# A hand-written start of a gated-attention and SiLU kernel: two weight pieces asked for ahead of the fourth chunk's loads, that chunk's transposes behind the third's scores, and two roundings ahead of Silus

## Chip, cores and metric

The kernel runs on one core of one Trainium2 chip. The metric is device time in microseconds (us), the median of several executions. The five engines of the core are named as in the profile: PE (TensorE; PEld are its weight loads), DVE (VectorE), ACT (ScalarE), POOL (GpSimd) and SP (SyncE, which here issues most DMAs; SPq are its issues).

## What is computed

A gated recurrence over 768 tokens for 4 x 8 heads of 48 columns, then a feed-forward block with SiLU over all 3072 tokens:

```python
batch, n_heads, seq, head_dim = (4, 8, 768, 48)
...
for t in range(S):
    state = alpha[:, :, t, :, None] * state + np.einsum('bhd,bhe->bhde', k[:, :, t], v[:, :, t])
    y[:, :, t] = np.einsum('bhd,bhde->bhe', q[:, :, t], state)
...
x = np.ascontiguousarray(attn_out.transpose(0, 2, 1, 3)).reshape(B * S, H * D)
...
h = x @ w_in                           # 3072x384 @ 384x2048
g = h * (1.0 / (1.0 + np.exp(-h)))
return (g @ w_out).astype(np.float32)  # 2048x384
```

Both weights arrive in 8-byte numbers, so the kernel reads them as pairs of 32-bit words ("bits") and makes single-precision weights of them itself.

## The kernel before

**Chunks.** The recurrence is worked in chunks of 128 tokens of one batch, all heads together; there are 24 (chunk 0 to 3 are the first 128 tokens of the four batches, chunk 4 starts the second 128 of batch 0). A chunk goes through these steps:

- `load(n)` (line 480) has SP issue three DMAs of 192 KB: alpha, k and q of the chunk (tiles `an`, `kn`, `qn`) into one of two sets of buffers, by n even or odd. `load_v(n)` (510) does the same for v (`vn`, two buffers).
- `bring(n)` (726) has PE transpose alpha, k and q, four transposes each, into PSUM, and ACT copies alpha's out (line 749, tile `al`). Alpha's bank, and from chunk 4 on k's and q's too, come from a pool of three, `ps_a`.
- `products(n)` (751) is DVE's part: two scans and two multiplies make the scaled k (`kp`) and q (`qp`, tile `p`).
- `scores(n)` (819) is 16 small matmuls into two banks of `ps_a`. ACT copies both out (line 844, tile `g`), POOL blanks the upper triangle (845), and `back` (871) transposes `kp` on PE, with a copy by ACT (881).
- `values(n)` (883) multiplies g with v, and ACT copies the result to `xt` (903), the input of the feed-forward block. `states(n)` (904) makes the state.

**Weights.** The 12 pieces of w_in (512 KB each) and then the 16 of w_out are fetched in order. `fetch()` (527) takes one of four buffers and has SP issue the DMA (533). `weights()` (629) turns one piece into single precision each time it is called: DVE, in three instructions (660, 662, 663), puts the number together, with a rounding that ACT has made ahead of it (644). Having done piece i, it issues the rounding of piece i + 1 on ACT and fetches piece i + 4. So each call to `w(upto)` in `start()` puts pieces through until `upto` of them are done. The buffer of piece i + 4 is that of piece i, which is free once DVE's line 662 and ACT's rounding have read it.

**Feed-forward block.** `go_on()` (1198) takes the next unit of work from a list. The first units are those of `enter_plain` (951): 12 matmuls of 128x256 with two column blocks of w_in into one of three banks (`ps_m`), then one Silu by ACT (963). The first four use pieces 0 to 5, the fifth and sixth pieces 6 to 8, and the seventh needs pieces up to 11.

**The order.** In `start()` (1237), which the change edits, the order of all this for the first chunks is written out by hand. The flag `stated` is on while it runs: PE's matmuls and transposes, the loads and fetches of SP, and ACT's roundings, Silus and copies are then kept in program order, each within its engine (lines 381 to 394). So what stands earlier in `start()` is issued earlier on each engine that it uses, and an instruction that waits holds up what follows on its own engine. After `start()`, a loop over steps with `fill` (1224) brings the remaining chunks and units.

Of the kernel before, what the change touches and what calls it, by code (L numbers as in the profile page):

```python
# [355 lines left out]
def quotients(  # L356
# [30 lines left out]
    def settled(ins):  # L387

        return tc.keep_in_program_order(ins) if stated[0] else ins
# [48 lines left out]
    def out_bank(i, n):  # L438
        return outs[i].tile([128, 512], F32, name="ps_o")[:, 0:n]

    def ps_attn(n=C):
        return ps_a.tile([128, 512], F32, name="ps_a").rearrange("p (j c) -> p j c", c=n)
# [4 lines left out]
    def idle(n):  # L447

        for _ in range(n):
            pe.matmul(spin[:, 0:C], lhsT=ident, rhs=ident, start=True, stop=True)  # L450
# [17 lines left out]
    NIN = 2  # L468
# [11 lines left out]
    def load(n, names="akq"):  # L480
        if n == NT:
            return
        c = ctxs.setdefault(n, dict(zip(("ci", "b"), divmod(n, B))))
        b, rows = c["b"], slice(c["ci"] * C, c["ci"] * C + C)
        for name, src in (("a", alpha), ("k", k), ("q", q)):
            if name not in names:
                continue
            x = src[b, :, rows, :]
            if n < NA:
                c[name] = nat[name][n % NIN]  # L490
                settled(nc.sync.dma_start(c[name][:, :, 0:D], x.transpose([1, 0, 2])))
                continue

            c[name] = late["quads"][name]
            for u in range(2):
                for i in range(2):
                    r = 64 * u + 32 * i
                    nc.sync.dma_start(  # L500
                        c[name][r : r + 32, 32 * (1 - i) :][:, 0 : 4 * NP * D].rearrange(
                            "p (g c) -> p g c", g=NP),
                        x[u::2].rearrange("h (b j) d -> b h (j d)", j=4))

    NV = 2
# [4 lines left out]
    def load_v(n):  # L510
        c = ctxs.setdefault(n, dict(zip(("ci", "b"), divmod(n, B))))
        x = v[c["b"], :, c["ci"] * C : c["ci"] * C + C, :].transpose([1, 0, 2])
        t = c["v"] = vns[n % NV]
        if n < NA:
            settled(nc.sync.dma_start(t[:, :, 0:D], x))
            return
        nc.sync.dma_start(t[:, 0 : H // 2, 0:D], x[:, 0 : H // 2])
        for e in range(2):
            nc.sync.dma_start(t[CH * e : CH * e + CH, H // 2 :, 0:D], x[CH - CH * e : C - CH * e, H // 2 :])
# [198 lines left out]
    def tokens(t):  # L718

        return t[:, 1 : NP * W + 1].rearrange("p (j c) -> p j c", c=W)[:, :, 0:C]  # L720

    def turned(x, to):
        x = x[:, 32:].rearrange("p (g j d) -> p g j d", j=4, d=D)
        dve.transpose(to.rearrange("p g (b j) -> p g j b", j=4), x[:, :, :, 0:32])

    def bring(n, names="akq"):

        c = ctxs[n]
        sg = seg[0 if late else n % 2]
        ps = c.setdefault("ps", {})  # L730

        for name in names:
            if n >= NA:
                if name == "a":
                    turned(c[name], tokens(sg))
                    load(n + 1, "a")
                continue
            if n < GB and name != "a":

                at = "kq".index(name)  # L740
                ps[name] = (bank(at) if n == 1 else out_bank(at, 512)).rearrange("p (j c) -> p j c", c=C)
            else:
                ps[name] = ps_attn()
            if n == 0 and name != "a" or n == 1 and name != "q":
                idle(2)
            for j in range(NP):
                pe.transpose(ps[name][:, j, :], c[name][:, 2 * j : 2 * j + 2, :], ident)
            if name == "a":
                settled(act.copy(tokens(sg), ps[name]))  # L749
# [69 lines left out]
    def scores(n):  # L819
        c = ctxs[n]  # L820
        ci, b = c["ci"], c["b"]
        ps = [ps_attn() for _ in range(2)]

        for j in (0, 2, 1, 3):
            for e in range(2 if n >= NA else 1):
                for u in range(2):
                    r = slice(64 * u, 64 * u + D)
                    at = slice(CH * e, CH * e + CH) if n >= NA else slice(0, C)  # L830
                    t = slice(CH * (e ^ j // 2) if n >= NA else 0, C)
                    pe.matmul(ps[u][at, j, t], lhsT=c["kp"][r, j, at], rhs=c["qp"][r, j, t],
                              start=True, stop=True)
        if n == 1:

            room = gpool.tile([128, 4, 2, TB], F32, name="g").rearrange("p a b n -> p (a b n)")
            c["room"] = room[:, 2 * NP * C :]
        g = (room[:, 0 : 2 * NP * C] if n == 1 else decayed).rearrange(
            "p (u j c) -> p u j c", u=2, j=NP)
        swapped = decayed.rearrange("p (o u j c) -> p o u j c", o=2, u=2, j=NP // 2)  # L840
        c["g"] = (lambda u, j: g[:, u, j, :]) if n < NA else (
            lambda u, j: swapped[:, j // 2, u, j % 2, :])
        for u in range(2 if n < NA else 0):
            settled(act.copy(g[:, u], ps[u]))
            gps.affine_select(g[:, u], g[:, u], pattern=[[0, NP], [1, C]], compare_op=ALU.is_ge,
                              fill=0.0, base=0, channel_multiplier=-1)
        if n >= NA:
            ps = [x.rearrange("p (o j) c -> p o j c", o=2) for x in ps]
            for u in range(2):
                act.copy(swapped[:, :, u, :, CH:], ps[u][:, :, :, CH:])  # L850
            for r, o in earlier:
                for u in range(2):
                    act.copy(swapped[r, o, u, :, 0:CH], ps[u][r, o, :, 0:CH])
            for at, half in ((CH, later), (0, earlier)):
                for r, o in half:
                    x = swapped[r, o].rearrange("p u j c -> p (u j) c")[:, :, at : at + CH]
                    gps.affine_select(x, x, pattern=[[0, NP], [1, CH]],  # L857
                                      compare_op=ALU.is_ge, fill=0.0, base=0, channel_multiplier=-1)
        if n != 1:
            back(n)  # L860
        if ci > 0:
            s = st[b].rearrange("p j u e -> p j (u e)")
            for j in range(NP):
                mul = act.mul(s[:, j], s[:, j], least[:, n, j : j + 1])
                if late:
                    tc.keep_in_program_order(mul)
# [81 lines left out]
    def bank(i, n=512):  # L948
        return banks[turn[i]].tile([128, 512], F32, name="ps_m")[:, 0:n]
# [203 lines left out]
    def convert(which, upto):  # L1153
        while conv_done[which] < min(upto, n_conv[which]):
            next(conv[which], None)
            conv_done[which] += 1
# [41 lines left out]
    def go_on():  # L1198

        nonlocal done  # L1200
        next(pieces[done][0], None)
        done += 1
# [34 lines left out]
    def start():  # L1237

        nonlocal bridged
        w = lambda upto: convert(0, upto)  # L1240
        products(0)
        products(1)
        load(NIN)
        next(conv[0])
        scores(0)
        w(1)
        idle(8)
        scores(1)
        values(0)
        back(1)  # L1250
        w(2)
        states(0)
        values(1)
        bridged = 2
        load_v(NV)
        w(3)
        load(NIN + 1)
        states(1)
        load_v(NV + 1)
        w(4)  # L1260
        bring(2, "a")
        w(5)
        go_on()
        bring(2, "kq")
        w(6)
        products(2)
        go_on()
        w(7)
        go_on()
        bring(3)  # L1270
        scores(2)
        w(8)
        go_on()
        w(9)
        values(2)
        states(2)
        load_v(NV + 2)
        load(NIN + 2)
        products(3)
        load(NIN + 3)  # L1280
        go_on()
        w(10)
        go_on()
        w(11)
        scores(3)
        bring(4)
        load(NIN + 4)
        values(3)
        bridged = 4
        w(12)  # L1290
        go_on()
        states(3)
        load_v(NV + 3)
        products(4)
        side_by_side(0, 0, 0)
        convert(1, 1)
        for _ in range(3):
            convert(1, 3 * (done - 6) // 2)
            go_on()
        stated.pop()  # L1300
        stated.append(False)
# [110 lines left out]
```

## Time and profile before

| | us |
|---|---|
| median of 3 runs | 555.82 |
| lowest and highest | 555.07, 556.57 |
| the profiled execution | 558.47 |
| its span, first to last instruction | 556.6 |
| PE busy in the span | 542.5 (97%) |
| DVE busy | 446.7 (80%) |
| ACT busy | 208.4 (37%) |
| POOL busy | 77.8 (14%) |

The page's slices divide the span into 40 equal parts of 13.9 us, each digit being tenths of that slice. The table of waits says who waited for whom and for how long in total. In a timeline, a line has its start, the time it covers, the engine, the line of the code, and in brackets how long the engine stood idle before and what released it. A line with x2 or more merges several instructions.

### The profile page before, as it was taken

The page shows a single profiled execution, that of the slowest core. Times are in us where ns is not written, and L with a number is a line of the kernel's source. Part 1 is how long each engine was busy: PE and PEld are TensorE (multiplying, and loading weights), DVE is VectorE, ACT ScalarE, POOL GpSimd, SP SyncE. Part 2 cuts the span into 40 slices and gives each one's busy share as a digit, 9 for nine tenths or more (in the row PEclk, how much of TensorE's full clock was granted, in tenths as well). Part 3 has the DMA queues.
Part 4 walks back from the last instruction along what each step waited for, and adds up shares of the span by engine and source line. Part 5 has one row for each costly group of instructions (what it writes and reads, how often), then busy time and mean ns, then how long its engine had stood idle before and what let it go on. Part 6 is the DMA issues. An engine that isn't in the chain of part 4 may idle for free. (4 is left out here: it accounts for less than half of the span.)

```text
span 556.6 us, 12718 instructions
## 1 busy us (share of the span) xinstructions
PE 542.5 (97%) x5068; PEld 494.4 (89%) x5068; DVE 446.7 (80%) x801; ACT 208.4 (37%) x466; POOL 77.8 (14%) x146
## 2 busy tenths in 40 slices
PE   8989999999999999999999999999999999999996
PEld 7768888898899999899999999988998999999996
DVE  5987698984899899997998986998984796955531
ACT  3535644223332253353353353353264332332200
POOL 4110000132210212021021021021121000001000
PEclk9979999999999999999999999999999999999999
DMA  9979871164454625355535744617652225500000
GB/s 213 251 246 187 231 193 46 50 160 124 112 134 119 162 65 138 90 133 151 136 106 154 194 125 136 171 49 183 164 143 84 61 71 180 161 32 15 16 26 28
DMA packets 99218, 70.11 MB, mean 126 GB/s; under 512 B 56272, under 2 KB 88656, under 8 KB 99152
## 3 DMA queue, kind: packets, MB, share of 16 engines
q1 hardware_dynamic: 97232, 65.30, 45.9%
q0 software_dynamic: 1920, 3.93, 2.0%
q8 instruction: 41, 0.67, 0.5%
q14 instruction: 25, 0.20, 0.1%
HBM read 61.34 MB, written 7.86 MB: 124 GB/s over the span
## 5 line engine op out<-in xcount | busy, mean ns | idle before, releaser
L394 PE MATMUL ps_o<-w_out,g 128*128 128x192 f32 x768 | 133.7, 328 | 0.0
L394 PEld LDWEIGHTS ps_o<-w_out,g 128*128 128x128 f32 x768 | 125.8, 190 | 2.5 <-issue 0.4
L394 PE MATMUL ps_m<-xt,w_in 128*128 128x256 f32 x480 | 114.6, 387 | 1.0 <-ACT xt L903 0.6
L394 PEld LDWEIGHTS ps_m<-xt,w_in 128*128 128x128 f32 x480 | 91.3, 193 | 14.3 <-ACT xt L903 0.8
L394 PE MATMUL ps_o<-wt,g 128*128 128x192 f32 x576 | 99.7, 326 | 0.0
L394 PEld LDWEIGHTS ps_o<-wt,g 128*128 128x128 f32 x576 | 95.1, 190 | 1.5
L394 PE MATMUL ps_m<-xc,w_in 128*128 128x256 f32 x288 | 70.7, 382 | 0.0
L394 PEld LDWEIGHTS ps_m<-xc,w_in 128*128 128x128 f32 x288 | 53.7, 190 | 7.0 <-DVE g L998 0.3
L995 ACT ACTIVATE g<-g 128x1024 f32<-128x1024 f32 x32 | 33.1, 1056 | 60.7 <-DVE g L998 60.6
L1087 DVE TENSOR_TENSOR g<-g 128x512 f32<-128x512 f32 x72 | 49.9, 705 | 6.9 <-PE ps_o L394 6.8
L857 POOL TENSOR_SCALAR_AFFINE_SELECT g<-g 64x256 f32<-64x256 f32 x64 | 35.1, 548 | 124.1 <-ACT g L850 105.4
L1099 POOL DMA_DIRECT2D out_dram<-o x40 | 22.1, 553 | 216.0 <-DVE o L1096 110.3
L394 PE MATMUL ps_m<-xc,wx 128*128 128x256 f32 x192 | 50.1, 383 | 1.0 <-DVE xc L600 1.0
L990 ACT COPY g<-ps_m 128x512 f32<-128x512 f32 x64 | 36.6, 588 | 37.0 <-PE ps_m L394 36.9
L394 PEld LDWEIGHTS ps_m<-xc,wx 128*128 128x128 f32 x192 | 35.2, 190 | 5.3 <-ACT u L1118 1.3
L998 DVE TENSOR_TENSOR g<-ps_m,g 128x512 f32<-128x512 f32 x56 | 36.9, 679 | 3.2 <-PE ps_m L394 2.7
L760 DVE TENSOR_TENSOR_SCAN u<-al,one 128x516 f32<-128x516 f32 x24 | 29.9, 1248 | 9.7 <-ACT al L749 9.4
L963 ACT ACTIVATE g<-ps_m 128x512 f32<-128x512 f32 x32 | 19.0, 595 | 42.4 <-PE ps_m L394 41.9
L990 ACT COPY part<-ps_m 128x512 f32<-128x512 f32 x32 | 18.9, 590 | 37.6 <-PE ps_m L394 24.0
L790 DVE TENSOR_TENSOR_SCAN p<-al,inv 128x516 f32<-128x516 f32 x24 | 29.9, 1247 | 1.0 <-PE ps_a L394 0.3
L713 DVE TENSOR_REDUCE seen<-bits 128x1 f32<-128x512 int32 (+1 forms) x33 | 26.3, 820 | 5.5 <-DMA bits<-in_moe_w_in_dram 5.5
L1096 DVE TENSOR_TENSOR o<-ps_o,u 128x192 f32<-128x192 f32 x24 | 8.4, 351 | 24.7 <-PE ps_o L394 22.8
(134 smaller groups left out, 654.3 us busy)
## 6 DMA issues: line engine op xcount, KB each, us to landing
bits<-in_moe_w_in_dram SPq DMA_DIRECT2D x24, 512.0 KB, 4.7
bits<-in_moe_w_out_dram SPq DMA_DIRECT2D x16, 384.0 KB, 3.8
at<-in_alpha_dram SPq DMA_DIRECT2D x64, 96.0 KB, 2.7
kt<-in_k_dram SPq DMA_DIRECT2D x64, 96.0 KB, 2.6
qt<-in_q_dram SPq DMA_DIRECT2D x64, 96.0 KB, 2.7
bits<-in_alpha_dram SPq DMA_DIRECT2D x9, 512.0 KB, 4.4
out_dram<-o POOLq DMA_DIRECT2D x40, 96.0 KB, 2.6
flips<-turn SPq DMA_DIRECT2D x12, 256.0 KB, 2.5
```

Source lines behind the costliest of these rows:

```text
L394: in_order(nc.tensor.matmul(*args, **kw))
L713: dve.tensor_reduce(seen[kind][which][:, i : i + 1], x, axis=AX, op=op, apply_absolute_value=True))
L760: settled(dve.tensor_tensor_scan(u[:, end - 1 :: -1], sg[:, end:0:-1], one[:, end:0:-1], 0.0, ALU.mult, ALU.add))
L790: settled(dve.tensor_tensor_scan(p[:, 0:end], sg[:, 0:end], iv[:, 0:end], 0.0, ALU.mult, ALU.add))
L857: gps.affine_select(x, x, pattern=[[0, NP], [1, CH]], compare_op=ALU.is_ge, fill=0.0, base=0, channel_multiplier=-1)
L963: settled(act.activation(gts[grp, h, pair][:, i : i + 2, q % 2, :], ps, AF.Silu))
L990: act.copy(to, ps)
L995: act.activation(x, x, AF.Silu)
L998: dve.tensor_tensor(to, a, b, op)
L1087: dve.tensor_tensor(cells(grp, h, pair, *to), cells(grp, h, pair, *x), cells(grp, h, pair, *y), ALU.subtract)
L1096: dve.tensor_tensor(o, x, y, ALU.add)
L1099: (gps if grp < NG - 1 else nc.sync).dma_start(out[r : r + C, c * HO : (c + 1) * HO], o)
```

## The change

Only `start()` is edited, and no instruction is added or taken out. The loads of chunk 3, with its v, come behind `w(4)` and `w(5)`, and so behind the fetches of w_in pieces 7 and 8, which these calls issue. The fourth unit of `go_on()` comes ahead of `scores(2)`, and `bring(3)` behind `scores(2)` and `w(8)`. The loads of chunk 4 come directly behind `w(7)`. The fifth unit comes behind `w(10)` and the sixth behind `w(11)`, and so behind the roundings of pieces 10 and 11 on ACT.

```diff
         bridged = 2
         load_v(NV)
         w(3)
-        load(NIN + 1)
         states(1)
-        load_v(NV + 1)
         w(4)
         bring(2, "a")
         w(5)
+        load(NIN + 1)
+        load_v(NV + 1)
         go_on()
         bring(2, "kq")
         w(6)
         products(2)
         go_on()
         w(7)
+        load(NIN + 2)
         go_on()
-        bring(3)
+        go_on()
         scores(2)
         w(8)
-        go_on()
+        bring(3)
         w(9)
         values(2)
         states(2)
         load_v(NV + 2)
-        load(NIN + 2)
         products(3)
         load(NIN + 3)
-        go_on()
         w(10)
         go_on()
         w(11)
+        go_on()
         scores(3)
         bring(4)
         load(NIN + 4)
```

`NIN` and `NV` are both 2.

## The prediction, made before the result was known

> **What bounds it now.** I read the page first. TensorE (PE) is busy 542.5 of 556.6 us, so only its idle time and slow clock can be saved. The slices show one dip of the granted clock, in the third (27.8 to 41.7 us, where `start()` orders the work by hand).
>
> ```profile
> PE   8989999999999999999999999999999999999996
> PEclk9979999999999999999999999999999999999999
> ```
>
> The waits between 28 and 36 us come next. The columns are the wait's total, its count and the longest.
>
> ```profile
> ACT up L644 <- DMA bits<-in_moe_w_in_dram: 7.0, 2, 4.5
> PE ps_a L398 <- ACT al L749: 2.4, 1, 2.4
> DVE w_in L660 <- DMA bits<-in_moe_w_in_dram: 0.6, 1, 0.6
> PE ps_o L398 <- DVE p L797: 0.4, 1, 0.4
> ```
>
> PE's 2.4 us are put down to the copy of alpha (al), but ACT itself stood 4.5 us in a rounding whose weight bits were not there. The timeline of ACT shows the queue behind it:
>
> ```profile
> 33.02 0.67 ACT L644 ACTIVATE up<-bits 128x512 int32<-128x512 uint32 x1 [4.50 <-DMA bits<-in_moe_w_in_dram]
> 33.59 0.58 ACT L963 ACTIVATE g<-ps_m 128x512 f32<-128x512 f32 x1
> 34.07 0.58 ACT L749 COPY al<-ps_a 128x512 f32<-128x512 f32 x1
> 34.54 1.09 ACT L844 COPY g<-ps_a 128x512 f32<-128x512 f32 x2
> ```
>
> The Silu at 33.59 belongs to matmuls that ended at 29.3; alpha's transposes ended at 29.8. Only the copy at 34.07 frees the score bank that PE wants at 32.3. SyncE's timeline tells why the bits were late:
>
> ```profile
> 19.98 0.35 SPq L533 DMA_DIRECT2D bits<-in_moe_w_in_dram  x1
> 20.38 0.72 SPq L491 DMA_DIRECT2D an<-in_alpha_dram  x1
> 21.15 2.48 SPq L491 DMA_DIRECT2D kn<-in_k_dram  x1
> 23.68 3.31 SPq L491 DMA_DIRECT2D qn<-in_q_dram  x1
> 27.09 0.67 SPq L515 DMA_DIRECT2D vn<-in_v_dram  x1
> 27.86 6.66 SPq L533 DMA_DIRECT2D bits<-in_moe_w_in_dram  x5
> ```
>
> Piece 6 (counted from 0) goes at 19.98, then chunk 3's four loads hold SP until 27.76, and piece 7, whose buffer VectorE (DVE) freed at 21.8, is asked for only at 27.86. It lands near 33. Last, a table of stretches (span, busy time and count of PE, PEld, DVE, ACT, POOL, clock, DMA share, GB/s):
>
> ```profile
> 31.75:34.70 2.95, 0.56 (x10) 0.36 (x9) 2.21 (x4) 1.68 (x4) 0.00 (x0) 0.84 0.99 394
> 34.70:40.40 5.70, 5.70 (x16) 4.58 (x16) 4.94 (x9) 2.08 (x4) 1.67 (x2) 0.50 0.66 227
> 40.40:42.10 1.70, 1.70 (x66) 1.29 (x64) 1.59 (x3) 1.24 (x3) 0.00 (x0) 0.95 0.00 0
> ```
>
> After the wait PE runs at half clock for 5.7 us: twelve 128x256 matmuls take 5.2 us where they take 2.76 at 20.5 us. The stall costs twice, and the DMA engines stand empty just after it (0.00 at 40.4 to 42.1).
>
> **What the Trainium skill says.** "TensorE: Matmul & The Clock Gate", Part 1: an idle window of about 3.4 us, free-running, halves the clock, and a busy one restores it. The half rate agrees; the edges near 33.7 and 40.4 lie about two windows apart; but the clock fell some 1.4 us after PE stopped, so a window that is half empty is enough (30.33 to 33.74 has PE 1.75 of 3.41 us busy). The same page, on engine queue depths, calls ScalarE strictly first in, first out: the block above agrees. "DMA: Bandwidth & Descriptors", on queues and rings, has descriptors consumed in ring order; piece 7 landing behind chunk 3 agrees. Its section on small descriptors makes them slow; here chunk loads (192-byte runs) move at about 160 to 195 GB/s (17 to 18 and 28 to 30 us), weight pieces at 350 to 420.
>
> **The change, part by part.**
>
> *Loads of chunk 3 behind pieces 7 and 8.* Four 192 KB DMAs move past two fetches on SP. Piece 7 can go at 21.85, piece 8 at 23.75 (piece 4's read ends at 23.69). By summing GB/s from 20 us I get the bytes: what is pending through piece 6 is 1.77 MB, moved by about 25.2 at the measured rates. At 0.36 MB/us piece 7 is through by 26.6 and piece 8 by 28.1; the landings here trail the bytes by 1.3 to 2 us, so 28.3 and 29.8 instead of 33 and later. This removes ACT's 4.5 us, PE's 2.4 and the slow clock. Chunk 3 pays: each load is 196 KB at 166 GB/s, 1.2 us. Alpha lands at about 31, k at 32.3, q at 33.8, v at 35, with 0.8 us for the gap that SP's blocked issue leaves at 27 us today. Bounds: q at 32.5 if there is no gap, at 37 if the blocked issues (2.5 and 3.3 us) leave twice as much.
>
> *Fourth `go_on` ahead of scores(2), `bring(3)` behind them.* Twelve matmuls and a Silu move up past 12 transposes, al's copy and the scores; nothing is added. DVE's order does not change. PE from 29.0: twelve matmuls at 0.21 us of weight load each, to 31.6; scores 1.1, to 32.7 (qp ready at 30.5, no wait); four kp transposes 0.45, to 33.2. `bring(3)` needs the first score bank copied: ACT, free after the fourth Silu at 32.5, copies g at 32.8 to 33.9; so transposes at 33.4, 33.85 and 34.3 to 34.7, q's being just in time. Here the cover is gone: the matmuls that hid ACT and POOL behind scores(2) are used up. The selects end at about 35.3 (chunk 0: copies from 12.06, selects done at 14.58), so values(2) waits 0.5 us. Without any cover (q at 37) it would be 2.5 us and a second slow clock. Values and states take 0.85 and 0.5: 36.7. DVE has piece 8 done at 36.1 (rounding 8 comes behind the copies, 35.2), so `go_on` five and six follow without a wait: 24 matmuls, 5.3 us, to 42.0.
>
> *scores(3)* then starts at 42.0 against 47.48: 5.5 us. products(3) is ready: al at 35.8, four DVE steps of 4.15 us altogether, 40.3. As a check, what vanishes is 2.4 + 0.4 idle and about 3.1 of slow clock (2.5 in the matmuls, 0.45 in the transposes), 5.9, less the new 0.5.
>
> *Roundings 10 and 11 ahead of Silus five and six.* No instruction more. DVE today waits 1.4 and 0.8 us for them (46.18, 48.78); that is hidden, at most 0.7 counts. But ACT is strict: queued behind rounding 11 are Silu six, the scores' copies, kn and al, and PE's transposes of chunk 4 wait for these banks.
>
> *Load(4) ahead of pieces 11 and 12.* Three DMAs move past two fetches and chunk 4's v; their buffers have been free since 24.2, and they fill an empty stretch. But piece 11 now stands behind 0.59 MB of short runs: 3 to 3.5 us. It landed at 38.5, and will at about 42 to 43.3, while ACT reaches rounding 11 at about 40.2. So ACT stands 2 to 3 us and Silu six ends at 43.3 to 44.3 instead of 42.5; copies, kn and al follow (1.07, 0.6, 0.6). Without that stall the selects would let values(3) begin 2.55 us after the scores end at 43.1, so at 45.7; with it, at 46 to 47. From below the cost is nothing (piece 11 at 41), from above 1.3 us. I take 46.6, a cost of 0.9. Today it begins at 50.93: a lead of 4.3 us.
>
> **After 52 us** nothing differs in order. DVE, ACT and DMA are ahead by about as much as PE (products(4): 46.6 against 50.81; the fetch of piece 13 at about 43 against 48.53), and PE idles under 1.9 us from 80 to 150, so the lead should last. Sum: lead 5.5 at scores(3); from there to values(3) 3.45 us today (47.48 to 50.93) and 4.6 then (42.0 to 46.6), 1.15 given back, of which 0.9 is piece 11; 4.3 in all. The profiled run took 558.47 (span 556.6) and would take 554.2; taken off the median of 555.82, 2.65 us below it, I get **551.5**.
>
> **The rivals.** *Second slow clock* (0.16). From 43 to 46.5 PE does only transposes and waits for ACT, about 2.2 us busy in a window of 3.4; 1.75 was too little at 33.7. If it drops there, 2.9 us are lost: gain 1.4, 554.4. For it: the thin stretch. Against it: such windows from 16.7 and 47.4, with PE 2.87 and 3.27 us busy, kept the clock.
>
> *Given back later* (0.12). DVE is busy 9.8 of 10 us from 100 to 110 and PE waits there for kp. If half of the gain ends there: 553.7. Against it: DVE's own queue moves earlier too.
>
> *Chunk 3 comes too late* (0.10, the slower side). Everything behind `bring(3)` moves with q's landing. With a stall above 1.5 us the clock falls (3 us more). Break-even: scores(3) at 47.5 less 42.0 less 3.0 leaves 2.5 us, so q at 36.8; from 38.5 it is slower by over 0.3%. At 39.5 it gives 558.5. For it: SP blocks in k and q, and landings took up to 7.6 us. Against it: q's request took 5.9 from issue to landing, and from about 27.5 that is 33.4.
>
> *It does not do what it says*: piece 7's buffer could come free late. DVE's read of piece 3 ended at 21.8, so no; I give it nothing.
>
> **How the numbers follow.** The main case has 0.62: 549.8 (neither new wait, 5.9) to 552.8 (both at their worst without a clock drop, about 3). The range 549.7 to 555.0 adds the first two rivals and leaves out chunk 3's lateness. Measurement tells 0.3% (1.7 us) from no change; faster means below 554.1. Faster: 0.62 + 0.08 + 0.04 = 0.74; the same: 0.12 + 0.04 = 0.16; slower 0.10.
>
> **What would show it.** Right: the rounding's 4.5 us gone, piece 7 asked for near 21.9, the clock at 1.00 from 34 to 40, scores(3) near 42, a new ACT wait for bits of 2 to 3 us near 41, values(2) waiting about 0.5 us for POOL. Wrong: PE waiting for an, kn or qn (chunk 3 late), a 0.5 in the clock between 43 and 50, or a lead at 52 us that is smaller at 150.

## The result, and the profile after

| | before | after |
|---|---|---|
| median of 22 executions each, us | 555.62 | 554.44 |
| lowest and highest, us | 554.20, 559.17 | 553.72, 555.27 |
| the profiled execution, us | 558.47 | 553.72 |
| its span, us | 556.6 | 552.0 |

The ratio is 0.9972, with a 95% interval of 0.9959 to 0.9984: faster by 1.2 us at the median (555.62 less 554.44), where 4.3 were forecast. That is just under the 0.3% that the prediction took as the least that can be told from no change, though the interval leaves 1 out. The two profiled executions lie 4.75 us apart (4.6 in their spans), close to the forecast. But the first lies 2.85 above the median of its kernel and the second 0.72 below its own; only the remaining 1.18 is between the medians. So the document has two questions: whether the steps in `start()` went as worked out, and why the medians show a quarter of it.

The page of the changed kernel, in slices. The clock's digit for the third slice is 9 now, where it was 7:

```profile
PE   8999999999999999999999999999999999999996
PEclk9999999999999999999999999999999999999999
```

SyncE's timeline of the changed kernel (start, time covered, engine, line). Pieces 6, 7 and 8 go out together ahead of chunk 3's loads, chunk 4's loads stand before piece 11 (37.03):

```profile
19.75 4.13 SPq L533 DMA_DIRECT2D bits<-in_moe_w_in_dram  x3
23.92 1.09 SPq L491 DMA_DIRECT2D an<-in_alpha_dram  x1
25.06 0.58 SPq L491 DMA_DIRECT2D kn<-in_k_dram  x1
25.68 3.50 SPq L491 DMA_DIRECT2D qn<-in_q_dram  x1
29.28 0.77 SPq L515 DMA_DIRECT2D vn<-in_v_dram  x1
30.16 1.58 SPq L533 DMA_DIRECT2D bits<-in_moe_w_in_dram  x2
...
37.03 0.80 SPq L533 DMA_DIRECT2D bits<-in_moe_w_in_dram  x1
```

Its waits between 28 and 48 us (total, count, longest). ACT's wait for bits is gone; a new one of 3.0 us has come, and PE waits 1.0 us behind it:

```profile
ACT up L644 <- DVE w_in L663: 3.0, 1, 3.0
PE ps_a L398 <- ACT g L844: 1.0, 1, 1.0
```

And its timeline, with lines of PE and ACT in order of time. The rounding at 28.24 is the one that came at 33.02 before; scores(3) begin at 42.09, where they began at 47.48 (the line of before stands with the first experiment); the Silu and copies behind the rounding at 43.16 are the new queue; values(3) begin at 46.43 (50.93 before):

```profile
28.24 0.67 ACT L644 ACTIVATE up<-bits 128x512 int32<-128x512 uint32 x1 [0.17 <-DVE inv L788]
...
31.84 1.16 PE L394 MATMUL ps_a<-p,kp 48*128 48x128 f32 x16
...
35.19 1.15 PE L394 MATMUL ps_a<-g,vn 128*32 128x128 f32 x30
...
42.09 1.16 PE L394 MATMUL ps_a<-p,kp 48*128 48x128 f32 x16
...
43.16 0.69 ACT L644 ACTIVATE up<-bits 128x512 int32<-128x512 uint32 x1 [2.96 <-DVE w_in L663]
...
43.74 0.59 ACT L963 ACTIVATE g<-ps_m 128x512 f32<-128x512 f32 x1
44.22 1.08 ACT L844 COPY g<-ps_a 128x512 f32<-128x512 f32 x2
...
44.87 0.66 PE L398 MATMUL ps_a<-ident,an 128*128 128x128 f32 x4 [1.03 <-ACT g L844]
...
46.43 1.08 PE L394 MATMUL ps_a<-g,vn 128*32 128x128 f32 x32
```

### The profile page after: what moved, and what is told of

It is laid out like the page before. It is cut to its first block, busy times and chain, and to the rows that moved or that the text cites. A ratio compares the mean times of both kernels' runs of the same rounds, so it can differ in the third digit from the quotient of the medians.

```text
span 552.0 us, 12718 instructions
## 1 busy us (share of the span) xinstructions
PE 539.4 (98%) x5068; PEld 491.9 (89%) x5068; DVE 446.9 (81%) x801; ACT 208.2 (38%) x466; POOL 79.0 (14%) x146
## 5 line engine op out<-in xcount | busy, mean ns | idle before, releaser
L394 PE MATMUL ps_m<-xt,w_in 128*128 128x256 f32 x480 | 111.9, 381 | 1.0 <-ACT xt L903 0.6
L394 PEld LDWEIGHTS ps_m<-xt,w_in 128*128 128x128 f32 x480 | 89.7, 190 | 13.6 <-ACT xt L903 0.8
L857 POOL TENSOR_SCALAR_AFFINE_SELECT g<-g 64x256 f32<-64x256 f32 x64 | 36.3, 567 | 124.1 <-ACT g L850 105.4
```

The costliest lines, as they stand in the source:

```text
L394: in_order(nc.tensor.matmul(*args, **kw))
L857: gps.affine_select(x, x, pattern=[[0, NP], [1, CH]], compare_op=ALU.is_ge, fill=0.0, base=0, channel_multiplier=-1)
```

## The experiments

Two theories stood against each other. **A, two clocks:** the slow clock that the profiled execution of the kernel before had is not in every execution, so its 3 us don't count in the median. **B, given back:** every execution has it, and ordinary ones lose the lead again later. In all comparisons the kernel before ran on the same chip, in turn with the other kernel, and a ratio is that of the medians of the two. An execution's mean clock is the share of full speed that PE was granted on average over it.

### The kernel before, again

No edit. 

> The kernel before, unchanged, so that each of its executions has its time beside its granted clock. Theory A (two clocks): the half clock after the wait at 32 to 35 us comes in a part of the executions only, as the free-running window happens to fall; the profiled one (558.47 us, clock 0.993) had it, the median one (555.6) has little of it. A expects times that spread from 554 to 559 and fall with the mean clock: near 554.5 where it is 0.998 or more, 557 to 559 where it is 0.993 or 0.994. Theory B (given back): every execution has the half clock and the 4.6 us lead of the changed kernel is lost again later. B expects a clock near 0.993 in all of them, with no tie between clock and time.

Measured: 554.93 (553.95 to 556.78, 14 executions) beside 46 more of the same kernel at 555.23. Each execution has its mean clock. The table has the executions of the kernel before that ran beside the other kernels, in three series, split by it; in each, nearly all times fall into two groups with little overlap:

| series | clock above 0.996: count, median (range) us | clock 0.996 or less: count, median (range) us |
|---|---|---|
| first | 34, 555.09 (553.68 to 556.14) | 12, 556.85 (556.20 to 557.26) |
| second | 48, 554.67 (553.76 to 555.79) | 15, 556.80 (556.36 to 557.99) |
| third | 44, 554.90 (553.66 to 555.91) | 14, 556.82 (555.79 to 557.78) |

Of the 14 of this run, one belongs to the second column (556.78 at 0.996). So the clock fell in 42 of 181 executions, about a quarter, and the two columns lie 1.8 to 2.1 us apart in their medians. None of the 181 reaches 558.47 at 0.993, the execution that was profiled first; among the 22 of the result, whose clocks were not recorded, three do or come near (558.44, 558.69, 559.17). A's form is right; its figure of 557 to 559 at 0.993 or 0.994 was too high for most, which have 0.995 or 0.996.

The profile of this repeat caught an execution in which the clock held. Its stretches (span, busy time and count of PE, PEld, DVE, ACT, POOL, clock, DMA share, GB/s) and PE's timeline:

```profile
33.00:34.00 1.00, 0.00 (x0) 0.00 (x0) 0.83 (x3) 1.00 (x3) 0.00 (x0) 1.00 1.03 414
36.00:37.00 1.00, 1.00 (x6) 0.89 (x5) 0.42 (x2) 0.36 (x1) 0.54 (x1) 1.00 0.79 299
40.00:41.00 1.00, 1.00 (x7) 0.87 (x6) 0.90 (x2) 0.00 (x0) 0.00 (x0) 1.00 0.84 173
```

```profile
34.36 0.66 PE L398 MATMUL ps_a<-ident,kp 128*128 128x128 f32 x4 [2.00 <-ACT al L749]
34.85 2.76 PE L394 MATMUL ps_m<-xt,w_in 128*128 128x256 f32 x12
...
44.27 1.16 PE L394 MATMUL ps_a<-p,kp 48*128 48x128 f32 x16
```

The same of the execution profiled at first:

```profile
33.00:34.00 1.00, 0.00 (x0) 0.00 (x0) 0.97 (x2) 0.98 (x2) 0.00 (x0) 0.87 1.03 422
36.00:37.00 1.00, 1.00 (x4) 0.77 (x3) 0.39 (x1) 1.00 (x2) 0.88 (x1) 0.50 0.87 328
40.00:41.00 1.00, 1.00 (x12) 0.46 (x14) 1.00 (x1) 0.14 (x1) 0.00 (x0) 0.71 0.07 19
```

```profile
34.70 1.11 PE L398 MATMUL ps_a<-ident,kp 128*128 128x128 f32 x4 [2.40 <-ACT al L749]
35.61 5.21 PE L394 MATMUL ps_m<-xt,w_in 128*128 128x256 f32 x12
...
47.48 1.16 PE L394 MATMUL ps_a<-p,kp 48*128 48x128 f32 x16
...
50.93 1.08 PE L394 MATMUL ps_a<-g,vn 128*32 128x128 f32 x32
```

The wait for al is there in both (2.00 and 2.40), and so is ACT's wait for bits (4.70 here). But the clock stays at 1.00, the twelve matmuls take 2.76 us and not 5.2, and scores(3) begin at 44.27 and not 47.48. How long the clock was down in the first profile follows from its slices, if it has only full and half speed: a mean of 0.87 from 33 to 34 puts the fall at 33.74, and 0.71 from 40 to 41 puts the return at 40.58, which is 6.84 us.

### Filling the wait

```diff
+        if n == 2:
+            spare = bank(0)
+            for _ in range(18):
+                pe.matmul(spare[:, 0:C], lhsT=ident, rhs=ident, start=True, stop=True)
         if n != 1:
             back(n)
```

> The kernel before with 18 extra 128x128 matmuls on PE between scores(2) and the four transposes behind them, about 2.1 us of work that is thrown away, in the place where PE waits 2.4 us; ACT's wait for weight bits stays. Only the slow clock can go. Theory A: the slow executions vanish and the fast ones stay as they are: median 554.5 to 555.0, spread under 2 us. Theory B: as every execution has the slow clock, all gain about 3 us: median 552.5 to 553.

Measured: 557.48 (557.23 to 557.64 and one at 558.11, 9 executions), ratio 1.0039 (1.0024 to 1.0054). I had the filler's cost wrong: each such matmul is two instructions in the trace, and 18 took 4.29 us, so PE ran 2 us past the end of the wait. The clock stayed above 0.996 in all nine and they lie close together. Less the 2 us this is near the kernel before with its clock held (555.09 in that series), but a number was missed, so I ran it again with eight.

> The kernel before with 8 extra 128x128 matmuls (thrown away) where PE waits 2 us ahead of the transposes behind scores(2). The 18 of the run before took 4.29 us, 0.24 each, and overran the wait by 2 us; 8 are 1.9 us and fit in. Theory A (two clocks, the clock falls in about a quarter of the executions): the slow quarter vanishes, the others stay, so median 554.8 to 555.4, all within 1.5 us, none above 556.

Measured: 555.32 (554.86 to 556.18, 14 executions), ratio 0.9994 (0.9980 to 1.0007). The eight take 2.05 us and `back`'s transposes follow at 34.33 without a wait:

```profile
32.44 2.05 PE L394 MATMUL ps_m<-ident 128*128 128x128 f32 x16
34.33 0.60 PE L398 MATMUL ps_a<-ident,kp 128*128 128x128 f32 x4
```

The lowest clock of the 14 is 0.997. One execution lies 0.18 above the bound that I gave; the median is as expected, though 0.65 above those executions of the kernel before in that series whose clock held (554.67), for which I have no explanation.

Together: with the wait of 2 us filled, the clock fell in none of 23. If it fell by chance in a quarter of them as before, none in 23 would come about twice in a thousand times. So the wait is what lets the clock fall. **B is out**: the clock falls in a part of the executions only, and a B kernel would have gained 3 us with the eight. Filling the wait has not made the kernel faster, though: the ratio of 0.9994 has 1 well inside its interval.

### Each part alone

The loads of chunk 3 behind pieces 7 and 8, with PE's old order:

```diff
-        load(NIN + 1)
         states(1)
-        load_v(NV + 1)
         w(4)
         bring(2, "a")
         w(5)
+        load(NIN + 1)
+        load_v(NV + 1)
```

> One part of the change alone: chunk 3's loads behind the fetches of pieces 7 and 8, everything else in the old order, so that its transposes still stand ahead of scores(2). Both theories: weight bits come in time and ACT's 4.5 us go, but PE stands at the transposes until q lands at about 34 (from 29.2): 4 us or more in place of 2.8, and the slow clock nearly always. Median 557 to 560.

Measured: 555.02 (553.89 to 558.88), ratio 0.9999 (0.9984 to 1.0014), a clear miss. PE's waits between 26 and 36 us in its profile, and the transposes of q:

```profile
PE ps_o L398 <- DVE w_in L660: 0.6, 1, 0.6
PE ps_o L398 <- DMA qn<-in_q_dram: 0.3, 1, 0.3
```

```profile
31.84 0.63 PE L398 MATMUL ps_o<-ident,qn 128*128 128x128 f32 x4 [0.27 <-DMA qn<-in_q_dram]
```

The transposes of q run at 31.84, so q landed 2 us sooner than the 34 that I reckoned with, and PE waits 0.9 us, not 4. The mean clock fell to 0.993 in one of 14 (558.88), though the profile of this kernel, taken of another execution, has no wait of PE above 0.6 us there; what that one execution waited for is not shown. Alone this part makes no difference that can be measured.

The order on PE and ACT, with the old loads:

```diff
         go_on()
-        bring(3)
+        go_on()
         scores(2)
         w(8)
-        go_on()
+        bring(3)
         w(9)
```

> The other part alone: the fourth go_on ahead of scores(2) and bring(3) behind them and piece 7's rounding, with all loads, the fifth and sixth go_on in their old places. ACT still waits for piece 7's bits to about 33, then does two Silus and the scores' copies to 35.4, so PE waits about 1.7 us ahead of chunk 3's first transposes. Theory A: 1 to 1.5 us behind the full change where the clock holds, 555 to 556, with some executions slower. Theory B: half clock in all, 557.

Measured: 554.48 (554.10 to 555.16, 22 executions), ratio 0.9983 (0.9974 to 0.9992), the clock at 0.997 or above in all. ACT still waits 4.6 us for piece 7's bits, and PE 1.3 us, in one place:

```profile
34.48 0.66 PE L398 MATMUL ps_a<-ident,an 128*128 128x128 f32 x4 [1.31 <-ACT g L844]
```

It lies 0.5 us below my expectation, and none of its executions was slower, as I had expected of some. The order alone has the whole effect of the change, to within the intervals: a shorter wait, with work on both sides, in which the clock did not fall in 22 executions.

### The new wait behind rounding 11

In the changed kernel ACT stands 3 us at rounding 11. I had forecast a wait of that size, for the bits of piece 11. The trace names DVE's line 663: there are two rounding buffers, and rounding 11 needs the one of rounding 9, which DVE reads only after products(3). Three kernels try this. In the first, the sixth unit's Silu is back ahead of the rounding:

```diff
         w(10)
         go_on()
-        w(11)
         go_on()
+        w(11)
         scores(3)
```

> The changed kernel with its last edit undone by half: the fifth and sixth go_on both stand behind w(10) and ahead of w(11), so rounding 10 stays ahead of its Silu and rounding 11 comes behind the sixth Silu. Theory U (rounding buffer): in the changed kernel rounding 11 waits 3.0 us on ACT for one of two rounding buffers, which DVE frees only behind products(3), and Silu, score copies and PE's transposes of chunk 4 stand behind it for 1.0 us. U expects this wait to go: 0.8 to 1.2 us less than the changed kernel, 553.2 to 553.6. Theory L (late piece 11, as I forecast): the wait is for the bits of piece 11, which come behind chunk 4's loads. L expects the same gain here.

In the second there are three buffers:

```diff
-    upp = first.enter_context(tc.tile_pool(name="upp", bufs=2))
+    upp = first.enter_context(tc.tile_pool(name="upp", bufs=3))
```

> The changed kernel with three rounding buffers in place of two, order as it is. Theory U: the 3.0 us wait of rounding 11 for DVE goes and only the landing of piece 11 (about 41.5) remains, PE no longer waits ahead of chunk 4's transposes: 553.2 to 553.8. Theory L: no difference, 554.4.

In the third, chunk 4's loads are back in their place:

```diff
         w(7)
-        load(NIN + 2)
         go_on()
...
         load_v(NV + 2)
+        load(NIN + 2)
```

> The changed kernel with chunk 4's loads back in their old place behind states(2), so that piece 11 is asked for right behind piece 10. Theory U: piece 11 lands 3 us earlier and nothing comes of it, 554.4, PE's 1.0 us wait ahead of chunk 4's transposes stays. Theory L: that wait goes, 553.2 to 553.6.

Measured: 554.18 (ratio 0.9980, 0.9970 to 0.9990), 553.91 (0.9971, 0.9958 to 0.9984) and 554.15 (0.9980, 0.9969 to 0.9991). Against the 554.44 of the result, from another series, none shows the 1 us of either theory. What ended ACT's wait in the changed kernel is U's: with chunk 4's loads in the old place ACT still waits for DVE, and with three buffers only the landing of the bits remains. But the late landing of L is there as well, and no later than I had forecast (42 to 43.3): with three buffers the bits hold the rounding until 42.43. In the changed kernel it is hidden, since the buffer comes free later, at 43.1. First the line of the kernel with chunk 4's loads back, then that of the one with three buffers:

```profile
42.94 0.68 ACT L644 ACTIVATE up<-bits 128x512 int32<-128x512 uint32 x1 [1.91 <-DVE w_in L663]
```

```profile
42.43 0.68 ACT L644 ACTIVATE up<-bits 128x512 int32<-128x512 uint32 x1 [1.39 <-DMA bits<-in_moe_w_in_dram]
```

PE's wait of 1.0 us is gone in all three profiles, also with the loads in the old place, where U had it stay. But values(3) begin at 46.53, 46.38 and 46.37 us in them, and at 46.43 in the changed kernel. To have the changed kernel on the same chip, and its wait again, I ran it once more, with three buffers beside it, and with three buffers and the old place of chunk 4's loads together.

> The changed kernel, unchanged, beside many executions of the kernel before with their clocks. Theory A: no execution of it has the slow clock in the body of the kernel; against those executions of the kernel before whose clock held it gains 0.5 to 0.8 us, against those with a mean clock of 0.996 or less 2.3 to 2.9 us; overall about 1.2 us.

> The changed kernel with three rounding buffers, on the same chip as the changed kernel this time. The profiles so far reach the transition from scores(3) to values(3) at the same 46.4 us with and without the wait for the buffer, since PE came there earlier in the one that waited. If the buffer costs something in most executions: 0.3 to 1.0 us less than the changed kernel; if the early arrival was a matter of that one execution: 0 to 0.3 us.

> Three rounding buffers and chunk 4's loads back behind states(2): no wait is left for rounding 11, neither the buffer nor the bits. 0 to 0.5 us less than the changed kernel; if it is the same as with three buffers alone, chunk 4's loads ahead of piece 11 cost nothing.

Measured: 554.31 (553.60 to 555.49; ratio 0.9982, 0.9973 to 0.9990), 554.19 (0.9984, 0.9976 to 0.9992) and 554.25 (0.9974, 0.9964 to 0.9984), 22 executions each. The changed kernel's wait of 1.0 us at chunk 4's transposes is there again, and absent in the other two. The medians differ by 0.12 and 0.06 us, too little to tell from nothing. Where it goes is only partly seen: with the wait, PE reaches scores(3) at 42.49, without it at 43.25 and 42.92. That the two are tied is not shown. No version beats the changed kernel, in the series in which both ran, by what can be measured.

Against the kernel before in that series, the changed one gains 0.83 us (555.14 less 554.31), against its executions with the clock held 0.59 (554.90) and against the others 2.5 (556.82). The last two are as expected; the first is less than the 1.2 that I named.

## Why the prediction was wrong

**The steps in the trace came out right.** Piece 7 is asked for near 22 us and its rounding is done by 28.9 without a wait for bits. The clock is at 1.00 from 34 to 40 us. Chunk 3 costs PE nothing: q's transposes follow at 34.66, and no wait for an, kn or qn is left. scores(2) begin at 31.84 (31.6 forecast), values(2) at 35.19 (35.3), scores(3) at 42.09 (42.0), values(3) at 46.43 (46.6). The forecast 0.5 us for POOL's selects did not appear; the line at 35.19 follows the transposes directly. None of the prediction's signs of being wrong appeared either: all of them were looked for in one profile, and the error lay between the profile and the median.

**One cause was misnamed.** ACT's 3 us at rounding 11 end with the rounding buffer, 0.7 us after piece 11's bits would have ended them (43.1 against the 42.4 of the kernel with three buffers). That the size was right is therefore in part luck. The cost of 0.9 that I put on it shows in the profile (1.0 of PE) but not clearly in the medians.

**The lead lasted.** Starts in us, from the two profiles of each kernel:

| | scores(3) | values(3) | scores(4) | last product | span |
|---|---|---|---|---|---|
| before, clock fell | 47.48 | 50.93 | 63.17 | 551.3 | 556.6 |
| before, clock held | 44.27 | 47.72 | 60.12 | 548.1 | 553.2 |
| after | 42.09 | 46.43 | 58.68 | 546.8 | 552.0 |
| after, again | 42.49 | 46.81 | 59.06 | 547.0 | 552.5 |

From values(3) on the lead of the first profile of after stays between 4.5 and 4.6 us over the first line and at 1.2 to 1.4 over the second. The other profile of after leads the second line by 0.9 to 1.1, and by 0.7 in the span. So what was gained at values(3) is not given back, or hardly.

**The step that failed** is the last of the sum: "taken off the median of 555.82, 2.65 us below it, I get **551.5**". The 5.9 us that "vanish" were 2.8 of idle time and 3.1 of slow clock (the two parts that it names for the clock, 2.5 and 0.45, make 2.95; the 549.8 that rests on the 5.9 should read 549.9). The slow clock belongs to the profiled execution, which had it for 6.8 us; of the 181 executions counted above, three quarters had their clock held. The last 0.8 of the idle time is that execution's too: where the clock held, PE waited 2.0 us. I had the sign in hand: the profiled execution lay 2.65 us above the median and outside the range of the three runs shown (555.07 to 556.57), and I took the difference for a constant to be carried over. It was most of the effect.

What is left for an execution with its clock held is the 2.0 us of waiting, less the new wait of 1.0. The profiles show about that at values(3), 1.3 and 0.9 us, and the medians 0.59. The 1.2 between the medians of the result is more than this, in part because executions with a fallen clock raise the median of the kernel before too (in the last series 555.14 with them, 554.90 without). Without the 3.1 of slow clock the prediction's own sum gives 5.5 − 3.1 = 2.4 at scores(3) and, less the 1.15 between there and values(3), about 1.2: 554.4 from the 555.62. That it meets the measured median is partly luck, since the sum is one for executions with the clock held.

The rival with the second slow clock names 554.4 as well, and that it meets the measured 554.44 is luck altogether: I asked whether the changed kernel would lose its clock, and not whether the kernel before always does. The changed kernel kept it (0.997 or above in all of 22 and 22 executions). What it does for the mean is therefore more than for the median, since the executions with a fallen clock are gone: in the last series 555.36 to 554.29.

## What to carry to other kernels

Before a saving from a profile is taken off a median, set the profiled execution's own time beside the median: if it lies outside the spread, find what that one execution had that others lack, and leave it out of the sum. A stretch at half clock after a wait is such a thing; its price in the mean is half its length times the share of executions in which it comes. Of the ways to keep the clock up here, putting real work into the wait, so that 1.3 us were left of 2.0, paid (ratio 0.9983); filling it with matmuls that are thrown away kept the clock up and gained nothing (0.9994).

## What the runs showed of the hardware

The same wait lets the clock fall in some executions only: in 42 of 181. "TensorE: Matmul & The Clock Gate" (Part 1 of that page of the Trainium skill) tells of a free-running window of about 3.4 us, one that does not start with the program. An outcome by chance would fit it, and the 6.84 us of the first profile are two such windows. But PE was idle for 2.40 us there and for 2.00 in the profile in which the clock held, so the longer wait may have decided; two profiles do not show which. The page speaks of an idle window; here PE was never idle for so long in the fallen profile, and the clock fell all the same.

The prediction's own rule, "With a stall above 1.5 us the clock falls", does not hold: with a stall of 2.00 us it stayed at 1.00. Nor does the busy share alone decide, as far as can be seen: in that execution PE was busy 1.41 of the 3.41 us from 30.95 to 34.36, less than the 1.75 before the fall. Where the edges of the windows lay is not shown.

None of the executions with 0.995 and 0.996 was profiled, so where and for how long their clock fell is not shown. An estimate from the clocks: they average 0.9952 to 0.9955 where the others average 0.9987 to 0.9990, and this difference, times a span of 553 us, is 1.8 to 2.1 us, as much as the medians differ. At half speed that is a fall of about 4 us, nearer to one window than to two.

Chunk loads were through sooner than a sum of bytes at the rate of before said: q at 31.84 in the kernel with only the loads moved, where I had 33.8. And two instructions stand in the trace for each matmul of 32-bit numbers in the code, with transposes left out: 16 took 2.05 us for eight of the filler, 36 took 4.29 for eighteen. So the "12 matmuls" of a unit and the "16" of the scores in the description of the kernel before are instructions, for 6 and 8 matmuls in the code.
